# Strided attention rows loaded as 64 + 8 instead of 72, into a larger ring, with more batches held ahead

## The chip, the cores and the metric

The kernel runs on one core of one Trainium2 chip. Times are device microseconds (us) of that core. Most runs of a kernel agree within some tenths of a per cent; runs over 1.5% above the fastest of the same kernel are called slow and left out of comparisons. A ratio of two kernels is the mean time of one kernel's fast runs over that of the other's of the same rounds, so it is not quite the ratio of the medians that stand beside it. Its 95% interval is given.

Positions inside a run ("at 71.86 us") are counted from the start of the profiled span.

## The reference, cut to what matters

Eight heads of attention over 576 positions, eight batches: heads 0 to 3 attend to the last 32 positions ("local"), heads 4 to 7 to the positions with the same remainder by 32 ("strided"). The result goes through a spectral layer with 64 complex modes, each with a real and an imaginary weight matrix of 512 x 512 in f32, and a last matrix.

```python
mask_local = (rel >= 0) & (rel < stride)
mask_strided = (rel >= 0) & (pos[None, :] % stride == pos[:, None] % stride)
...
X = np.fft.rfft(x, axis=1)
Yr = einsum('bmd,mde->bme', Xr, w_r) - einsum('bmd,mde->bme', Xi, w_i)   # 64 modes
Yi = einsum('bmd,mde->bme', Xr, w_i) + einsum('bmd,mde->bme', Xi, w_r)
u = x + irfft(Y);  out = u + maximum(u @ w_ch, 0)
```

The weights are 134 MB of the 163 MB that the kernel reads. They are read once, in two halves (128 tiles, each for one mode and one half of the channels).

## The kernel before

GpSimd issues all large loads; they turn f32 into f16 on the way. In order of time: eight strided batches, eight local batches with the first 64 modes between their pieces, then the second 64 modes with the turns and premixes of the output, then the output.

```python
NWBUF = 12                                   # weight tiles
pin = tile_pool(name="pin", bufs=3)          # three batches of q, k, v

def load(i):                                 # i < 8: strided batch i; else local batch i - 8
    qn = pin.tile([128, 3, 2048], F16, tag="qn")
    for vi, src in ((2, v), (0, q), (1, k)):
        if i < B:      # 4 heads x 18 = 72 rows of 32 x 64 f32
            nc.gpsimd.dma_start(qn[0:72, vi, :],
                src[i, 4:8].rearrange("h (c r) d -> (h c) (r d)", r=32))
        else:          # 128 rows of 18 x 64
            nc.gpsimd.dma_start(qn[:, vi, 0:1152],
                src[i - B, 0:4].rearrange("h (cb i) d -> (h cb) (i d)", i=18))
...
load(0); load(1); load(2); w_fetch(2)
for b in range(B):                           # strided stage
    load(b + 3)
    w_fetch([3, 3, 2, 2, 2, 2, 1, 1][b])
    ...
for b in range(B):                           # local stage, with modes of the first half
    load(B + b + 3)
    ...
```

A mode multiplies with its tile and then fetches the tile that will take its place; modes 3 to 6 sit in guest tiles and fetch nothing. In the second half the turns and premixes ("work") lie between the modes, two a mode over the last `LATE` modes:

```python
LATE = 10
first = len(work) - 2 * LATE
for m in range(NM - 3):
    mode(1, m)                               # 16 matmuls with the weight tile, then w_fetch()
    if m < NM - 3 - LATE:
        upto = -(-first * (m + 1) // (NM - 3 - LATE))
    else:
        upto = first + 2 * (m - (NM - 4 - LATE))
    for w in work[n:upto]:
        w()
    ...
```

The softmax here doesn't subtract the row's maximum and nothing guards it: scores larger than these inputs give would overflow.

## Time and profile before

| | before |
|---|---|
| time, median of 4 runs | 443.22 us (442.81 to 445.03) |
| span of the profiled run | 440.9 us |
| last strided load landed | 74.96 us |
| last weights landed | 402.17 us |
| from there to the end | 38.75 us |

The landings are read from the trace: each load makes sixteen completions, read here as one for each of the sixteen DMA engines, and has landed with the last. The two landings divide the run. Up to 74.96 us the strided loads and the first weight tiles are moved, up to 402 the rest of the stream, and then only the output is left. The prediction below shows the slices, the windows and the chain of waits of this kernel.

### The profile page before, as it was taken

To read this page: it belongs to the slowest core of one execution; us is meant where nothing else is said; L and a number is where in the kernel's file an instruction comes from. 1 tells how busy PE (TensorE), PEld (TensorE's weight loads), DVE (VectorE), ACT (ScalarE), POOL (GpSimd) and SP (SyncE) were. 2 spreads that over 40 slices of the span, in tenths; PEclk is the share of its full clock that TensorE was granted. 3 is DMA by queue.
4 is the path that set the end of the run, shared out by engine and by line. 5 is a ranking of instruction groups with operands and counts; after the bars stand their busy time and mean duration, and the time that the engine had idled before them with its cause. 6 is when DMAs were issued, how large, how long until landed. Compare 5 with 4: busy or idle time off the path is not lost.

```text
span 440.9 us, 12290 instructions
## 1 busy us (share of the span) xinstructions
PE 335.6 (76%) x5284; PEld 240.4 (55%) x5284; DVE 215.9 (49%) x462; ACT 188.7 (43%) x353; POOL 181.1 (41%) x327
## 2 busy tenths in 40 slices
PE   2887778769899897875885567777685858987994
PEld 2766667648778765664663344444453535654441
DVE  3787868644435434150511034344334442763894
ACT  1685767554545553342441302123313402443882
POOL 5333333432544343533443443433434444420883
PEclk9998989697958995585865559596869778999999
DMA  8999999999999999999999999999999999992687
GB/s 186 183 201 201 200 196 204 211 211 208 198 211 212 211 212 212 212 211 212 213 210 211 212 211 213 213 211 212 211 198 207 213 211 212 212 212 44 263 329 268
DMA packets 30902, 92.35 MB, mean 209 GB/s; under 512 B 5952, under 2 KB 6848, under 8 KB 30848
## 3 DMA queue, kind: packets, MB, share of 16 engines
q0 software_dynamic: 26608, 81.28, 94.3%
q1 hardware_dynamic: 3440, 9.50, 5.7%
q8 instruction: 42, 0.69, 0.6%
q10 hardware_dynamic: 800, 0.77, 0.6%
q14 instruction: 12, 0.10, 0.1%
HBM read 163.37 MB, written 9.44 MB: 392 GB/s over the span
## 4 chain that ended last, share of the span: by engine, by line
DMA 58%; PE 28%; DVE 6%; issue 4%; ACT 3%; DVEq 0%; POOL 0%; POOLq 0%; ACTq 0%
DMA wt<-in_moe_w_i_dram 38%; DMA wt<-in_moe_w_r_dram 9%; DMA qn<-in_v_dram 5%; PE y L515 4%; DMA qn<-in_q_dram 4%; PE tp L363 3%; PE sc L613 2%; DMA qn<-in_k_dram 2%; PE v L860 2%; PE u L663 2%; PE v L648 2%; PE sc L409 1%; PE sc L482 1%; DVE xb L218 1%; PE sc L425 1%
## 5 line engine op out<-in xcount | busy, mean ns | idle before, releaser
L515 PE MATMUL y<-X,wt 128*128 128x16 f16 (+1 forms) x2048 | 82.8, 192 | 63.2 <-DMA wt<-in_moe_w_i_dram 60.1
L180 POOL DMA_DIRECT2D wt<-in_moe_w_r_dram x128 | 66.4, 519 | 131.0 <-DMA wt<-in_moe_w_r_dram 29.6
L515 PEld LDWEIGHTS <-wt 128*128 128x128 f16 (+1 forms) x2048 | 72.1, 103 | 76.7 <-issue 56.1
L180 POOL DMA_DIRECT2D wt<-in_moe_w_i_dram x126 | 65.3, 518 | 61.8 <-DMA wt<-in_moe_w_i_dram 38.8
L622 ACT ACTIVATE v<-sc 128x512 f16<-128x512 f32 x32 | 19.0, 597 | 88.8 <-PE sc L613 88.8
L613 PE MATMUL sc<-w_cp,xT 128*128 128x512 f16 (+1 forms) x160 | 49.8, 439 | 0.5 <-DVE xT L585 0.4
L439 ACT ACTIVATE PL<-sc 128x480 f16<-128x480 f32 (+1 forms) x48 | 27.6, 579 | 38.4 <-PE sc L425 38.0
L623 DVE COPY xo<-tp 128x512 f16<-128x512 f16 x32 | 22.1, 692 | 39.4 <-PE tp L621 39.4
L218 DVE TENSOR_TENSOR xb<-av,rec 90x256 f16<-90x256 f32 (+2 forms) x80 | 36.0, 450 | 2.8
L217 DVE RECIPROCAL rec<-av 90x4 f32<-90x4 f32 (+2 forms) x80 | 14.7, 184 | 43.0 <-PE av L454 30.1
L370 DVE COPY qT<-tp 128x576 f16<-128x576 f16 x16 | 12.1, 759 | 45.1 <-PE tp L363 45.1
L228 ACT ACTIVATE v<-tp 128x640 f16<-128x640 f16 (+1 forms) x24 | 19.4, 808 | 26.1 <-PE tp L397 22.8
L363 PE MATMUL tp<-cI_s,qn 64*64 64x64 f16 x864 | 27.5, 216 | 3.6 <-DMA qn<-in_q_dram 2.2
L328 ACT ACTIVATE PS<-sc 90x360 f16<-90x360 f32 (+1 forms) x48 | 22.7, 489 | 9.6 <-PE sc L321 9.2
L363 PEld LDWEIGHTS <-qn 64*64 64x64 f16 x864 | 21.8, 128 | 8.8 <-issue 3.5
L873 POOL TENSOR_TENSOR rl<-rl,xo 128x512 f32<-128x512 f32 x16 | 18.3, 1158 | 18.2 <-ACT rl L871 17.8
L890 DVE TENSOR_TENSOR osb<-u,rl 128x512 f32<-128x512 f32 x36 | 23.9, 689 | 2.5 <-PE u L663 0.7
L409 PE MATMUL sc<-cMl_s,cI_s 128*128 128x480 f16 (+1 forms) x48 | 22.6, 471 | 1.6 <-ACT X L228 1.6
L253 PE MATMUL tp<-cI_s,qn 72*128 72x72 f16 x256 | 14.8, 207 | 11.8 <-DMA qn<-in_v_dram 9.1
L482 PEld LDWEIGHTS <-xb 108*128 108x128 f16 (+2 forms) x176 | 17.3, 115 | 11.8 <-DVE xb L218 6.1
L425 PE MATMUL sc<-qT,kz 128*128 128x160 f16 (+1 forms) x160 | 22.7, 269 | 0.0
L565 DVE COPY xT<-tp 128x512 f16<-128x512 f16 x16 | 11.0, 689 | 23.4 <-DMA wt<-in_moe_w_i_dram 14.2
(94 smaller groups left out, 639.4 us busy)
## 6 DMA issues: line engine op xcount, KB each, us to landing
wt<-in_moe_w_r_dram POOLq DMA_DIRECT2D x128, 256.0 KB, 9.4
wt<-in_moe_w_i_dram POOLq DMA_DIRECT2D x126, 256.0 KB, 9.7
out_dram<-osb SPq DMA_DIRECT2D x14, 512.0 KB, 2.7
qn<-in_v_dram POOLq DMA_DIRECT2D x16, 288.0 KB, 10.7
qn<-in_q_dram POOLq DMA_DIRECT2D x16, 288.0 KB, 10.7
qn<-in_k_dram POOLq DMA_DIRECT2D x16, 288.0 KB, 11.0
out_dram<-osb SPq DMA_DIRECT2D x7, 128.0 KB, 2.5
out_dram<-osb SPq DMA_DIRECT2D x3, 256.0 KB, 3.2
```

The lines of the kernel that those rows point to most:

```text
L180: nc.gpsimd.dma_start(wt[ds(64 * ri, 64)], src[m, ds(256 * half, 256), :].rearrange("(p c) e -> p c e", c=4),)
L218: nc.vector.tensor_tensor(out=dst, in0=val.rearrange("p h (q c) -> p h c q", c=4), in1=rec[0:n, 0:pieces] .to_broadcast((n, pieces, 64)) . ...
L328: nc.scalar.activation(out=PS[0:n, ds(POFF[t], 4 * n)], in_=scp[0:n, 0 : 4 * n], func=ACTF.Exp, scale=SCALE,)
L363: nc.tensor.transpose(tp[ds(64 * hp, 64), ds(64 * i, 64)], qn[ds(64 * hp, 64), vi, ds(64 * (9 * g + i), 64)], idn[ds(64 * hp, 64), ds(64 * ...
L409: nc.tensor.matmul(scp[:, 0 : n * times].rearrange("p (h x) -> p h x", h=times), idn, mask_rows("cMl", n, times), start=True, stop=False,)
L425: nc.tensor.matmul(scp[:, ds(col, n)], kzs[par][:, hp, ds(s0, 128)], qTs[par][:, ds(s0, n)], start=False, stop=(i == len(todo) - 1),)
L439: nc.scalar.activation(out=dst, in_=src, func=ACTF.Exp, scale=SCALE)
L482: nc.tensor.matmul(xp[:, ds(192 * cp, 192)], xb[b][0:n, base + t, ds(128 * cp, 128)], F[0:n, t, :], start=(i == 0), stop=(i == len(tiles) ...
L515: nc.tensor.matmul(yv[:, mi, e, :], wt[pr, XC[c], ds(128 * e, 128)], Xh[half][pr, c, :, :, m], start=(c == 0), stop=(c == 3),)
L613: nc.tensor.matmul(vp[pr, :], xT[:, ch, cols], w_chs["cp"][:, ch, :], start=(ch == 0), stop=(ch == 3),)
L623: nc.vector.tensor_copy(out=xo[pr].rearrange("p (h q c) -> p h q c", h=2, c=4), in_=tp[pr, 0:512].rearrange("p (h c q) -> p h q c", h=2, c=4),
L890: nc.vector.tensor_tensor(out=osb[:, t % 2, :], in0=up, in1=rls[b, t][:, t % 2, :], op=AluOp.add)
```

## The change

Its intent: to give each DMA engine the same share of a strided load, and to keep more loads in hand. A strided tensor comes as 64 rows of its batch; its last 8 rows come with those of the next batch in one load of 8 partitions x 2 rows (here called the tail), every second batch. All of it lies in one ring of 12 tensors (four batches); local batches use two ring places each, six of them ahead. For the room, a weight tile is given up and the strided probabilities (PS) lie inside the local ones (PL), which costs one more fill with zeros.

```diff
-NWBUF = 12
+NWBUF = 11
...
-    PS = pat.tile([128, 2342], F16, name="PS")
+    PS = PL[:, ds(PS0, 2342)]
+    ring = pat.tile([128, 12, 2048], F16, name="ring")
...
+    def load_str(b):
+        for vi in (2, 0, 1):
+            nc.gpsimd.dma_start(
+                str_in(b, vi)[0:64],
+                SRC[vi][b, 4:8].rearrange("h (c r) d -> (h c) (r d)", r=32)[0:64],
+            )
+            if b % 2 == 0:
+                n = 3 * (b % 4) + SLOT[vi]
                 nc.gpsimd.dma_start(
-                    qn[0:72, vi, :],
-                    src[i, 4:8].rearrange("h (c r) d -> (h c) (r d)", r=32),
+                    ring[64:72, n : n + 4 : 3, :],
+                    SRC[vi][b : b + 2, 4:8].rearrange(
+                        "b h (c r) d -> (h c) b (r d)", r=32
+                    )[64:72],
                 )
...
-        load(b + 3)
-        w_fetch([3, 3, 2, 2, 2, 2, 1, 1][b])
+        if b < 5:
+            load_str(b + 3)
+        load_loc(*[(), (), (), (), (0,), (1, 2), (3,), (4, 5)][b])
+        w_fetch([3, 3, 2, 2, 2, 1, 1, 1][b])
...
-        load(B + b + 3)
+        load_loc(b + 6)
```

More of the change, by code (lines that the diff above doesn't have):

```diff
@@ L146 @@
     actx = ctx.enter_context(ExitStack())
-    pin = actx.enter_context(tc.tile_pool(name="pin", bufs=3))
+    pin = actx.enter_context(tc.tile_pool(name="pin", bufs=1))
     pat = actx.enter_context(tc.tile_pool(name="pat", bufs=1))
+    ring = pat.tile([128, 12, 2048], F16, name="ring")
     qTs = [pat.tile([128, 1152], F16, name=f"qT{i}") for i in range(2)]
@@ L152 @@
     vT = pat.tile([128, 1216], F16, name="vT")
-    PS = pat.tile([128, 2342], F16, name="PS")
     PL = pat.tile([128, 4160], F16, name="PL")
+    PS0 = 4160 - 2342
+    PS = PL[:, ds(PS0, 2342)]
     v16 = [pat.tile([128, 12, 132], F16, name=f"v16_{i}") for i in range(2)]
     GUEST = {3: ("Y0", 0), 4: ("Y0", 1), 5: ("X0", 0), 6: ("X0", 1)}
-    GUEST |= {16: ("YT", 0), 17: ("YT", 1)}
+    GUEST |= {15: ("YT", 0), 16: ("YT", 1)}
     guests = {}
@@ L189, in w_ch_fetch, with str_in, loc_in, load_loc @@
         w_chs["n"] = w_ch
-    qns = {}
-    def load(i):
-        if i >= 2 * B:
-            return
-        qn = pin.tile([128, 3, 2048], F16, tag="qn", name="qn")
-        for vi, src in ((2, v), (0, q), (1, k)):
-            if i < B:
+    SRC = {2: v, 0: q, 1: k}
+    SLOT = {2: 0, 0: 1, 1: 2}
+    def str_in(b, vi):
+        return ring[0:72, 3 * (b % 4) + SLOT[vi], :]
+    def loc_in(b, vi):
+        t = ring[:, ds(2 * (b % 6), 2), :].rearrange("p n x -> p (n x)")
+        return t[:, ds(1152 * vi, 1152)]
+    def load_str(b):
[6 more added lines that the diff above has]
+                n = 3 * (b % 4) + SLOT[vi]
                 nc.gpsimd.dma_start(
-                    qn[0:72, vi, :],
-                    src[i, 4:8].rearrange("h (c r) d -> (h c) (r d)", r=32),
-                )
-            else:
+                    ring[64:72, n : n + 4 : 3, :],
+                    SRC[vi][b : b + 2, 4:8].rearrange(
+                        "b h (c r) d -> (h c) b (r d)", r=32
+                    )[64:72],
+                )
+    def load_loc(*bs):
+        for b in bs:
+            if b >= B:
+                return
+            for vi in (2, 0, 1):
                 nc.gpsimd.dma_start(
-                    qn[:, vi, 0:1152],
-                    src[i - B, 0:4].rearrange("h (cb i) d -> (h cb) (i d)", i=18),
+                    loc_in(b, vi),
+                    SRC[vi][b, 0:4].rearrange("h (cb i) d -> (h cb) (i d)", i=18),
                 )
-        qns[i] = qn
     def v_cols(i):
@@ L233, in str_q @@
     def str_q(b, g):
-        qn, qT = qns[b], qTs[b % 2]
+        qn, qT = str_in(b, 0), qTs[b % 2]
         tp = psum("tp", half=True)
@@ L238, in str_q @@
                 tp[:, ds(72 * i, 72)],
-                qn[0:72, 0, ds(128 * (8 * g + i), 128)],
+                qn[:, ds(128 * (8 * g + i), 128)],
                 idn[0:72, 0:72],
@@ L247, in str_turn @@
     def str_turn(b, vi, j):
-        qn = qns[b]
+        qn = str_in(b, vi)
         a, z = JG[j]
@@ L254, in str_turn @@
                 tp[:, ds(72 * i, 72)],
-                qn[0:72, vi, ds(128 * (a + i), 128)],
+                qn[:, ds(128 * (a + i), 128)],
                 idn[0:72, 0:72],
@@ L358, in loc_turn @@
     def loc_turn(b, vi, g):
-        qn, par = qns[B + b], b % 2
+        qn, par = loc_in(b, vi), b % 2
         tp = psum("tp", half=True)
@@ L364, in loc_turn @@
                     tp[ds(64 * hp, 64), ds(64 * i, 64)],
-                    qn[ds(64 * hp, 64), vi, ds(64 * (9 * g + i), 64)],
+                    qn[ds(64 * hp, 64), ds(64 * (9 * g + i), 64)],
                     idn[ds(64 * hp, 64), ds(64 * hp, 64)],
@@ L676 @@
     psum_pools(tp=3, sc=3, av=2)
-    load(0)
+    load_str(0)
     const_load(nc.scalar, "cI", "cM6", "cM5", "cFs")
-    load(1)
+    load_str(1)
     const_load(nc.sync, "cMl", "cFl", "cA")
-    load(2)
+    load_str(2)
     w_fetch(2)
@@ L733 @@
         if b == 1:
-            nc.vector.memset(PL, 0.0)
+            nc.vector.memset(PL[:, 0:PS0], 0.0)
     str_values(B - 1, 4)
     str_values(B - 1, 5)
+    nc.vector.memset(PS, 0.0)
     dft(B - 1, 1)
```

## The prediction

> **What bounds the kernel now.** I read the page first (slices, chain), then the chain in order of time, then the busy time in windows, and last the completions of single loads in the trace.
>
> ```profile
> DMA  8999999999999999999999999999999999992687
> GB/s 186 183 201 201 200 196 204 211 211 208 198 211 212 211 212 212 212 211 212 213 210 211 212 211 213 213 211 212 211 198 207 213 211 212 212 212 44 263 329 268
> ...
> DMA 58%; PE 28%; DVE 6%; issue 4%; ACT 3%; DVEq 0%; POOL 0%; POOLq 0%; ACTq 0%
> ```
>
> Each slice is 11.0 us. The DMA is at 9 tenths in all slices from the second to the 36th, and the chain of waits is 58% DMA. The rate is 210 to 213 GB/s (bytes written to SBUF, half of what is read, since the loads turn f32 into f16) on most of the way, but 183 to 204 in the first seven slices, which are the strided attention. The windows show it finer (last columns: granted clock, DMA share, GB/s):
>
> ```profile
> 40.00:50.00 10.00, 8.56 (x159) 7.15 (x157) 8.27 (x25) 8.06 (x17) 3.79 (x8) 1.00 1.03 198
> 50.00:60.00 10.00, 7.78 (x142) 6.50 (x143) 8.29 (x23) 7.95 (x19) 3.66 (x7) 1.00 1.03 200
> 60.00:70.00 10.00, 7.51 (x111) 6.57 (x111) 6.33 (x18) 5.72 (x13) 3.71 (x8) 0.83 1.03 197
> ...
> 80.00:90.00 10.00, 7.35 (x147) 6.37 (x147) 6.90 (x17) 4.87 (x10) 3.79 (x8) 0.66 1.08 210
> ...
> 110.00:120.00 10.00, 9.06 (x210) 7.36 (x210) 5.00 (x10) 5.48 (x11) 5.77 (x11) 1.00 1.03 196
> 120.00:130.00 10.00, 9.03 (x182) 7.70 (x183) 3.48 (x8) 4.52 (x7) 4.15 (x8) 0.60 1.09 212
> ```
>
> DMA share 1.03 against 1.07 to 1.09 means that some of the 16 DMA engines stand idle in the strided stage, although loads are always queued. The chain in time says what the end hangs on:
>
> ```profile
> 71.86 10.22 DMA qn<-in_q_dram
> 82.12 1.17 PE tp L363 x36
> ...
> 147.62 9.85 DMA wt<-in_moe_w_r_dram
> ...
> 361.70 9.63 DMA wt<-in_moe_w_i_dram
> 371.46 0.65 PE y L515 x16
> 372.11 0.86 PE sc L613 x4
> ```
>
> Up to 82 us it is mostly loads, from 82 to 147 PE (local attention with the first modes), from 147 to 371 weight loads alone, then compute with the last modes. Setting each mode's first matmul beside the landing of its weights: mode 0 starts 75 us after its weights landed, mode 33 1.7 us, and from mode 34 (158.7 us) to the end of the stream most start within 0.05 to 0.7 us of the landing. So the PE-bound stretch is absorbed by the weights held ahead, and what sets the end is **when the load stream has moved all its bytes**. The last weights land at 402.2 us, and 38.7 us of modes, spectra and output follow.
>
> **How a strided load runs.** Completions of each load, read one by one from the trace: a load counts 16 completions. Of the eight strided loads issued first, the eighth gets its first completion at 7.3 us, its second at 11.1, and the other fourteen between 18.8 and 19.7. One engine gets none of the 72 rows, one gets two, fourteen get five each: 14 x 5 + 2 = 72. A weight load (64 rows of 4 KB) completes every 1.237 us, four rows an engine, so 0.309 us a row. An even strided load would take 72 / 16 x 0.309 = 1.39 us; five rows are 1.55. From 59.65 to 69.42 us three strided and four weight loads end: (9.77 - 4 x 1.24) / 3 = 1.60 us each. The uneven shares thus cost about 1.60 - 1.39 = 0.21 us x 24 loads = **5.1 us**. The light engines can't use the time: GpSimd's loads signal eight semaphores in turn, and each waits for the load eight before it, so no more than eight are outstanding.
>
> **What the Trainium skill says.** "DMA: Bandwidth & Descriptors", section "Why a DMA increments its semaphore by 16 and not by 1": as a rule the engine count k is the largest number up to 16 that divides the slowest dimension, the k engines being taken from a round-robin cursor; but GpSimd gives some copies k = 16 with partitions/16 rounded up per engine. The trace agrees with the exception: 72 rows go as 14 x 5 + 2 (the rule would give 12 x 6). For the new tail load, whose slowest dimension is 8, the rule gives eight engines in rotation, the exception one partition each on the same eight; no load of the kernel before has that shape. "SBUF — State Buffer", section "Door 1: The DMA port swizzle": partitions 64 to 67 share one of 16 write ports, 68 to 71 another, about 27 GB/s each. Nothing in this trace isolates that: the 64-row weight loads, which that page confines to eight ports (about 218 GB/s), reach 212 but alternate between halves.
>
> **The change, part by part.**
> - *64 rows.* Each of 24 main loads has four rows an engine, like a weight load: 24 x 1.24 = 29.8 us of stream.
> - *Tails.* 12 loads of 8 partitions x 2 rows of 4 KB. Spread or rotated they cost 16 rows / 16 x 0.309 = 0.31 us on average, 3.7 in all; with main loads 33.5, against 24 x 1.60 = 38.4 now: **-4.9 us**. Always on the same eight engines they cost 2 rows, 0.62 us, 7.4 in all: 37.2, only **-1.2 us**, since those eight would carry 4 + 4 + 2 = 10 rows per pair and tensor, as fourteen carry now.
> - *GpSimd issue.* 12 more at 0.53 us, 6.4 us; GpSimd is 41% busy and waits for the semaphores anyway: nothing.
> - *Ring of four batches instead of three.* A strided load no longer waits for the batch just transposed. Those waits did not empty the queue (eight outstanding), so nothing on its own.
> - *Six local batches ahead, one weight tile less.* Before the first refill there are now 17 tiles and 6 batches instead of 18 and 4: two batches (3 loads x 1.40 us each) more, one tile (2.47 us) less, 5.9 us more work in hand. Now there is a pause of issues, 104.7 to 110.0 us (modes 3 to 6 free no tile), and completions slip there: 196 instead of 212 GB/s for 10 us, **0.75 us**. With more queued it should go. The weights of modes 30 to 50 come later relative to the locals, but the sum at mode 63 is the same. Total bytes do not change. Eleven tiles are still far more than the four that eight outstanding loads fill.
> - *PS inside PL.* One fill of 2342 columns at the stage's end; 4160 columns take 1.79 us now, so about 1.0 us on DVE (38% to 69% busy from 80 to 100 us), in the stretch that the held weights absorb: nothing.
>
> Sum: 4.9 + 0.75 = 5.65 us if the tails rotate, 1.95 us if they do not. At the end everything hangs on the stream: mode 115 starts 0.14 us after its landing, and from there the compute chain has its fixed length, so a gain of the stream is passed on whole.
>
> **Rivals.**
> 1. *Tails always on the same eight engines*: 443.3 - 2 = 441.4. For it: the 72-row loads follow the rounding exception. Against: the tail has another form (two counts, 8 and 2).
> 2. *The two ports of partitions 64 to 71 hold up the tails.* By that page's rate, 64 KB over 2 x 27.2 GB/s is 1.2 us a tail instead of 0.31, if all engines write it at once: up to 12 x 0.9 = 10.7 us lost, so 443.3 - 5.65 + 10.7 = 448. Against: engines are spread by 2 to 8 us between first and last completion of a load, and an average over a pair of batches is far under the ports' rate. I take part of it, perhaps 1 to 2 us.
> 3. *Compute takes over.* In the strided stage DVE and ACT are at about 80%; if the stage can't run faster, the loads still run ahead into ring and weight tiles, so it becomes the end only if PE stays behind past mode 34. Then the time is 443. Against: PE is only 71% busy from 200 to 250 us.
> 4. *The loads in a wrong order or a hidden wait between them*: neighbouring loads into one tensor with a stride of three slots might be ordered behind each other's landing (about 10 us each, six or eight times, with an emptied queue): 460 or more. Nothing in the profile speaks for it.
>
> **Range and chances.** Rotation (-5.65) and fixed engines (-2) about evenly, a little less for ports: -4.3, so 439.0. The best case with the other start-up slack gone (the first 20 us at 184 GB/s also carry the constants) is about -8, 435.3; a full port loss partly paid back, or compute taking over, gives 443.5. A gain over 2% would need -8.9 us, more than the losses that I find in the stage: 6%. Slower by 2% needs the fourth rival or the full second one: 2%.
>
> **What would show it.** Right: the first seven slices near 208 to 212 GB/s, DMA share 1.07 in windows of the strided stage; main loads completing every 1.24 to 1.3 us; no dip at 110 us; the last weights landing at about 398 us with the same 38 to 39 us after it; weights as the main part of the chain from about 150 us. Tails on eight fixed engines would show as the share staying near 1.04 and eight early completions per load. Ports would show as tails whose packets take well over the 0.32 us of a 4 KB row now. The prediction is wrong if GpSimd waits for landings of tails, if the stage after 98 us leaves the DMA idle, or if the stretch after the last landing grows.

## The result, and the profile after

The changed kernel takes 438.94 us (median of 4 runs, 438.3 to 439.67) against 443.22; the ratio is 0.9896 (0.9865 to 0.9928). Two later comparisons gave 0.9888 and 0.9916. The forecast was 439.0.

The slices and the chain of the changed kernel's page:

```profile
DMA  8999999999999999999999999999999999990687
GB/s 186 211 211 212 211 213 209 211 210 211 213 211 212 213 208 211 213 212 211 211 212 211 213 212 210 213 213 210 201 211 212 211 212 213 211 192 15 264 324 277
...
DMA 74%; PE 15%; DVE 4%; issue 4%; POOL 1%; ACT 0%; DVEq 0%; POOLq 0%
```

The stage that ran at 183 to 204 GB/s runs at 209 to 213 from the second slice on, and the dip near 110 us (198) is gone. The thirty-sixth slice has begun to empty (192) and the thirty-seventh stands at 15, where it was 212 and 44: the stream ends earlier. The windows that answer to those in the prediction:

```profile
40.00:50.00 10.00, 7.83 (x146) 6.58 (x144) 8.35 (x23) 7.46 (x18) 4.68 (x10) 1.00 1.07 213
50.00:60.00 10.00, 7.98 (x147) 6.59 (x143) 8.30 (x24) 8.00 (x18) 4.88 (x10) 1.00 1.06 211
60.00:70.00 10.00, 8.08 (x148) 6.72 (x145) 8.27 (x24) 7.92 (x18) 4.59 (x9) 1.00 1.07 210
...
110.00:120.00 10.00, 8.67 (x249) 7.39 (x241) 5.84 (x10) 5.74 (x11) 3.98 (x8) 1.00 1.07 213
```

The DMA share (next to last column) is 1.06 to 1.07 where it was 1.03. Over the whole run PE, DVE and ACT are busy for 338.0, 215.6 and 188.6 us, where it was 335.6, 215.9 and 188.7: the same compute, better fed.

Below are the landings of both kernels, in us.

| | before | after | gain |
|---|---|---|---|
| last strided load landed | 74.96 | 70.14 | 4.8 |
| weights of mode 115 landed | 371.33 | 366.52 | 4.8 |
| last weights (mode 127) landed | 402.17 | 396.36 | 5.8 |
| first matmul of mode 127 | 402.41 | 399.05 | 3.4 |
| span | 440.9 | 437.8 | 3.1 |

So the stream gained 4.8 us in the strided stage, still 4.8 at mode 115 and 5.8 at its end (the prediction's favourable case was 5.65), and the kernel did not get all of it. Before, the last mode started 0.24 us after its weights. Now it starts 2.7 us after them: PE and DVE are behind. (The profiled run of the changed kernel, 439.67 us, was the slowest of its four; that of the kernel before took 442.69. So the spans are 3.1 us apart and the medians 4.3.) The chain of the changed kernel in time, cut to where this happens:

```profile
366.65 0.65 PE y L536 x16
...
387.27 1.22 PE sc L634 x3
388.49 0.43 PE tp L642 x4
388.91 0.47 PE y L536 x16
389.39 1.71 PE sc L634 x4
391.10 0.22 PE tp L642 x4
391.32 0.86 PE sc L634 x4
```

From 366.65 us (mode 115) on, no load is in the chain: it is the modes (L536), the premixes (L634, L642) and DVE's copies. The chain was as long as that before, too (30.95 us from mode 115 to mode 127, now 32.40). The difference is the clock: the premix matmuls at 387 and 389 us take 1.22 and 1.71 us, those at 391 us 0.86. The two stretches as windows, first the kernel before and then the changed one:

```profile
371.40:402.40 31.00, 27.02 (x354) 17.69 (x355) 18.97 (x39) 11.85 (x20) 8.78 (x17) 1.00 0.95 189
```

```profile
366.60:399.10 32.50, 28.57 (x356) 18.31 (x357) 18.91 (x38) 11.84 (x20) 8.76 (x17) 0.95 0.88 176
```

PE is busy for 27.02 us at a granted clock of 1.00 in the one and for 28.57 us at 0.95 in the other. A repeat of the changed kernel drew 0.95 again (32.4 us), another 1.00 (31.0 us):

```profile
367.60:398.60 31.00, 27.12 (x354) 17.76 (x355) 19.29 (x39) 11.92 (x21) 8.76 (x17) 1.00 0.92 184
```

Ten fast profiles have this stretch with the same work in it. In five the clock is 1.00 and it takes 30.9 to 31.0 us, in the other five the clock is 0.95 and it takes 32.4 to 32.6, whether the stream ends at 396 or at 402 us. So which clock it gets is chance, as far as these runs show.

Even at full clock the chain of 31 us is longer than the 29.7 us in which twelve tiles come (two loads of 1.237 us each). Before, that did not show at the last mode: the stream stumbled twice in its last 16 us (two loads landed 2.10 and 2.69 us after their predecessors instead of 1.24) and ended no earlier than the compute. Its chain has no load after mode 115 either. So of the 5.8 us, 1.0 is only that these late loads are missing now, in a stretch where compute sets the end. The 4.8 us that the stream had gained by mode 115 are passed on, less 1.45 us for the clock: 3.4. Why the two loads came late is not known; the other two profiles with whole 72-row loads need 30.7 and 30.9 us for the twelve tiles too, the other fast ones 29.7 to 29.9.

### The profile page after: what moved, and what is told of

It is laid out like the page before. It is cut to its first block, busy times and chain, and to the rows that moved or that the text cites. A ratio compares the mean times of both kernels' runs of the same rounds, so it can differ in the third digit from the quotient of the medians.

```text
span 437.8 us, 12314 instructions
## 1 busy us (share of the span) xinstructions
PE 338.0 (77%) x5284; PEld 240.9 (55%) x5284; DVE 215.6 (49%) x463; ACT 188.6 (43%) x353; POOL 186.8 (43%) x339
## 4 chain that ended last, share of the span: by engine, by line
DMA 74%; PE 15%; DVE 4%; issue 4%; POOL 1%; ACT 0%; DVEq 0%; POOLq 0%
DMA wt<-in_moe_w_i_dram 54%; DMA wt<-in_moe_w_r_dram 12%; DMA ring<-in_v_dram 4%; DMA ring<-in_q_dram 4%; PE sc L634 3%; PE v L884 2%; PE v L669 2%; PE u L684 2%; PE y L536 1%; DVE yy L663 1%; PE u L903 1%; PE tp L313 1%; POOL wt L183 1%; PE tp L642 1%; DVE xT L586 1%
## 5 line engine op out<-in xcount | busy, mean ns | idle before, releaser
L536 PE MATMUL y<-X,wt 128*128 128x16 f16 (+1 forms) x2048 | 82.2, 192 | 59.0 <-DMA wt<-in_moe_w_i_dram 57.1
L536 PEld LDWEIGHTS <-wt 128*128 128x128 f16 (+1 forms) x2048 | 72.0, 103 | 72.7 <-issue 51.7
L634 PE MATMUL sc<-w_cp,xT 128*128 128x512 f16 (+1 forms) x160 | 52.5, 459 | 0.5 <-DVE xT L606 0.4
L349 ACT ACTIVATE PL<-sc 90x360 f16<-90x360 f32 (+1 forms) x48 | 22.8, 490 | 9.8 <-PE sc L342 9.1
L384 PE MATMUL tp<-cI_s,ring 64*64 64x64 f16 x864 | 26.1, 211 | 1.0 <-DVE qT L391 0.6
L384 PEld LDWEIGHTS <-ring 64*64 64x64 f16 x864 | 20.7, 123 | 6.2 <-issue 3.4
L634 PEld LDWEIGHTS <-xT 128*128 128x128 f16 (+1 forms) x160 | 14.8, 110 | 14.9 <-issue 7.2
L446 PEld LDWEIGHTS <-kz 128*128 128x128 f16 x160 | 16.7, 118 | 11.3 <-issue 8.8
L274 PE MATMUL tp<-cI_s,ring 72*128 72x72 f16 x256 | 15.1, 207 | 10.1 <-DMA ring<-in_v_dram 7.7
## 6 DMA issues: line engine op xcount, KB each, us to landing
ring<-in_q_dram POOLq DMA_DIRECT2D x8, 288.0 KB, 10.7
```

The lines of the kernel that those rows point to most:

```text
L349: nc.scalar.activation(out=PS[0:n, ds(POFF[t], 4 * n)], in_=scp[0:n, 0 : 4 * n], func=ACTF.Exp, scale=SCALE,)
L384: nc.tensor.transpose(tp[ds(64 * hp, 64), ds(64 * i, 64)], qn[ds(64 * hp, 64), ds(64 * (9 * g + i), 64)], idn[ds(64 * hp, 64), ds(64 * hp, ...
L446: nc.tensor.matmul(scp[:, ds(col, n)], kzs[par][:, hp, ds(s0, 128)], qTs[par][:, ds(s0, n)], start=False, stop=(i == len(todo) - 1),)
L536: nc.tensor.matmul(yv[:, mi, e, :], wt[pr, XC[c], ds(128 * e, 128)], Xh[half][pr, c, :, :, m], start=(c == 0), stop=(c == 3),)
L634: nc.tensor.matmul(vp[pr, :], xT[:, ch, cols], w_chs["cp"][:, ch, :], start=(ch == 0), stop=(ch == 3),)
```

## The experiments

Twelve runs were made, on several chips; each is compared with the kernel before on its own chip (median 443.7 to 444.2 us). All results were correct. The table has what the profiled run of each shows, with the row packet's mean over 20 to 75 us (a row of 2048 f16 is one packet of 4096 bytes; in the two kernels with two pieces these are the rows of weights alone, as a strided row makes two packets there).

| run | median us | ratio (95%) | last strided landing | mean packet, ns | last weights landed | last mode behind them |
|---|---|---|---|---|---|---|
| before (first profile) | 443.22 | 1 | 74.96 | 335.8 | 402.17 | 0.24 |
| changed, again | 439.23 | 0.9888 (0.9862 to 0.9914) | 69.89 | 324.2 | 396.18 | 2.80 |
| changed, third | 439.39 | 0.9916 (0.9888 to 0.9944) | 70.19 | 324.1 | 397.15 | 1.47 |
| 72 rows in the ring | 443.49 | 0.9988 (0.9964 to 1.0013) | 75.10 | 332.1 | 401.86 | 1.96 |
| split only | 442.17 | 0.9959 (0.9936 to 0.9982) | 72.72 | 332.1 | 399.40 | 1.37 |
| one-row tails | 441.68 | 0.9946 (0.9924 to 0.9969) | 72.70 | 333.8 | 399.33 | 1.35 |
| dummies between tails | 444.41 | 1.0001 (0.9968 to 1.0033) | 77.41 (slow run) | 339.3 (slow run) | 403.93 (slow run) | 3.60 (slow run) |
| changed, even spread | 437.49 | 0.9853 (0.9828 to 0.9878) | 69.55 | 324.3 | 395.95 | 0.13 |
| before, even spread | 443.47 | 0.9985 (0.996 to 1.0011) | 74.34 | 332.5 | 402.03 | 0.14 |
| two pieces | 443.76 | 1.0007 (0.9987 to 1.0027) | 75.20 | 346.1 | 401.74 | 2.94 |
| two pieces, even spread | 442.73 | 0.9989 (0.9973 to 1.0006) | 76.68 | 346.5 | 403.21 | 0.13 |
| locals as before | 441.18 | 0.9961 (0.9921 to 1.0) | 70.07 | 324.2 | 398.44 | 1.36 |
| 80 rows | 442.01 | 0.9938 (0.9892 to 0.9984) | 72.35 | 324.2 | 399.22 | 2.80 |

### The changed kernel again

> The changed kernel itself, once more, beside the others on one chip. Measured before: 438.94 us against 443.22, and in its profile the last weights land at 396.36 us against 402.17 (5.8 us earlier), but the last mode starts 2.7 us after its weights landed instead of 0.24. Theory A (the stream's gain is steady, the loss after it is how fast PE runs in the last 30 us): again 438 to 440 us, last landing 396 to 397, last mode 2 to 4 us behind it. Rival (the profiled run was unlucky): last mode less than 1 us behind, and the time nearer to 437.

> The changed kernel, to be compared on one chip with the three kernels beside it: 438 to 440 us, last landing about 396 us, last mode 2 to 4 us behind it.

The stream ends at 396.18 and 397.15 us and the last mode is 2.80 and 1.47 us behind. The two runs differ in the granted clock of the last stretch (0.95 and 1.00), as told above. The loss at the end is steady, its size is not; the rival (under 1 us behind) is out.

### The split undone

```diff
             nc.gpsimd.dma_start(
-                str_in(b, vi)[0:64],
-                SRC[vi][b, 4:8].rearrange("h (c r) d -> (h c) (r d)", r=32)[0:64],
+                str_in(b, vi),
+                SRC[vi][b, 4:8].rearrange("h (c r) d -> (h c) (r d)", r=32),
             )
-            if b % 2 == 0:  ... (the tail)
```

> The changed kernel with the 64 + 8 split undone: each strided tensor comes as one load of 72 rows again, everything else (ring of four batches, six local batches ahead, 11 weight tiles, fill of PS at the end of the stage) is kept. Theory A (the even shares carry the gain): strided loads complete every 1.6 us again, 40 to 80 us is back at about 200 GB/s, the last weights land at 401 to 402 us, time 441.5 to 443.5; the pause near 110 us stays away, worth 0.75 us. Rival B (the gain is the ring and the work in hand): last landing stays near 397 and the time at 439.

443.49 us, a ratio of 0.9988: no different from the kernel before. The stage from 20 to 70 us, first the changed kernel and then this one:

```profile
20.00:70.00 50.00, 39.96 (x697) 33.58 (x695) 40.74 (x112) 38.19 (x83) 23.31 (x45) 0.97 1.06 211
```

```profile
20.00:70.00 50.00, 40.46 (x681) 33.38 (x679) 39.14 (x108) 37.11 (x80) 19.15 (x37) 0.93 1.03 201
```

211 GB/s falls back to 201, and the last landings of both kinds are those of the kernel before within 0.3 us. So ring, six batches and eleven tiles bring nothing by themselves; the split carries the gain. Rival B is out.

### The split alone, with tails of one row

```diff
-                nc.gpsimd.dma_start(
-                    qn[0:72, vi, :],
-                    src[i, 4:8].rearrange("h (c r) d -> (h c) (r d)", r=32),
-                )
+                rows = src[i, 4:8].rearrange("h (c r) d -> (h c) (r d)", r=32)
+                nc.gpsimd.dma_start(qn[0:64, vi, :], rows[0:64])
+                nc.gpsimd.dma_start(qn[64:72, vi, :], rows[64:72])
```

> The kernel before with only the loads split: 64 rows, then 8 rows of the same batch, into its own three tiles, 12 weight tiles, locals as before. Theory A: the strided stage runs at 208 to 212 GB/s, last landing 4 to 5 us earlier than before (397 to 398 us), the pause of issues near 105 to 110 us is still there (it may cost more, as less or no more work is in hand), time 439 to 440.5. Rival B (ring and work in hand): no earlier than 401 us, time 442 to 443.5.

The gain is about half of what I expected: 442.17 us, last landing 399.40. The old kernel can't hold the tails of two batches at once, so each tail has eight rows of one batch here. The next run shows that it is this form, and not the missing ring, that halves the gain.

### One-row tails in the changed kernel

```diff
-            if b % 2 == 0:
-                n = 3 * (b % 4) + SLOT[vi]
-                nc.gpsimd.dma_start(ring[64:72, n : n + 4 : 3, :], ... )
+            nc.gpsimd.dma_start(
+                str_in(b, vi)[64:72],
+                SRC[vi][b, 4:8].rearrange("h (c r) d -> (h c) (r d)", r=32)[64:72],
+            )
```

> The changed kernel with 24 tails of 8 rows of one batch instead of 12 of 8 x 2 rows. If eight engines are taken in turn, two tails of one row do what one of two rows does: last landing within 0.5 us of the changed kernel, time within 0.7 us (438.3 to 439.7), with 12 more issues that cost nothing. Rival (a tail costs a fixed time per load, or always lies on the same engines): 12 more tails at 0.3 us each, last landing 3 us later or more, time about 441.

441.68 us and a last landing at 399.33, 3.15 us later than in the changed kernel on the same chip: the first theory falls and the rival's number stands. The completions of a 64-row load tell which of the rival's two reasons is right. They are listed from the trace; the last of the four lines is the first load of a later experiment.

```
kernel, load issued at            its sixteen completions (us)
before, 5.04                      7.32, 11.07, then fourteen from 18.81 to 19.67
changed, 12.25 (64 rows)          sixteen from 17.82 to 19.48, no gap over 0.37
one-row tails, 13.45 (64 rows)    eight from 17.67 to 17.79, eight from 18.86 to 19.38
two pieces, 1.35 (72 rows)        four from 4.89 to 5.14, twelve from 6.52 to 7.49
```

With one-row tails the engines fall into two groups of eight, one group ahead of the other, and the distance from first to last completion grows to 4.0 us by the 18th tensor. The distance falls to 2.3 to 3.1 us for the last six tensors. A cost per load would hit all engines alike. So tails of one row fall on the same eight engines each time, which then have 4 + 1 = 5 rows for every tensor, as fourteen engines had before. The tails of 8 x 2 rows do not: with 12 of them the spread stays between 1.5 and 2.9 us through the stage, and the stage ends 2.8 us earlier. Always on the same eight, 12 tails of two rows would cost those eight just what 24 of one row do.

That is the prediction's favourable case by its effect, but a tail spread over all sixteen engines, a row each, would have the same effect. The trace does not name the engine of a packet; still, the completions tell the two apart. With one-row tails the first completion of a tail comes 0.15 to 0.19 us after the first of its main load, in 23 of 24 tails: the engine that is ahead never gets a row of the tail. With two-row tails it comes, from the third to the twelfth, 0.17, 0.50, 0.17, 0.50, 0.18, 0.62, 0.18, 0.59, 0.21 and 0.57 us after it: the engine that is ahead gets no row and two rows in turn. The four other profiles with the changed kernel's strided loads alternate as well. So the engines change from tail to tail.

### Dummies between the tails

```diff
+    scr = pat.tile([128, 12, 16], F16, name="scr")
...
+                nc.gpsimd.dma_start(
+                    scr[0:8, 3 * (b // 2) + SLOT[vi], :], v[0, 0, 0:8, 0:16]
+                )
```

> The changed kernel with a dummy load of 8 rows of 64 bytes after each tail, into a scratch tensor that nothing reads. If the eight engines of a load are taken from a cursor that moves on by eight, the dummies take one half of the engines each time and all real tails fall on the other half: those carry 4 + 4 + 2 = 10 rows per pair of batches and tensor, 2 rows more than if alternated over two tails as 1 on average, 12 x 0.31 = 3.7 us of stream. Expected then: completions of one load spread over 4 us and more by the end of the strided stage (2.2 us in the changed kernel), rate near 203 to 206 GB/s, last landing at about 400 us, time 441.5 to 443. Rival (the tail's 16 rows lie on all 16 engines, or always on the same eight whatever comes between): landing within 0.7 us of the changed kernel's 396.4, time within 1 us of it.

This run does not answer its question. It is as slow as the kernel before (ratio 1.0001), but probably not by the reason that it was to test: the dummies have the one-row form, which by the run above does not move on, and they fill the queue. GpSimd waits for the load eight before, and with a tail and a dummy after each main load only two or three of those outstanding from 17 to 20 us are main loads. The engines then seem to run dry: the load issued at 19.56 us lands on all sixteen engines within 0.81 us, as after a pause. Its profile: slow (448.7 us), so its landings are not compared, and that the full queue costs the time is not shown. It does show that small loads take places in the queue of eight.

### 72 rows in two pieces

```diff
-    ring = pat.tile([128, 12, 2048], F16, name="ring")
+    ring = pat.tile([128, 12, 2080], F16, name="ring")
...
+                ring[0:72, 3 * (b % 4) + SLOT[vi], :].rearrange(
+                    "p (k x) -> p k x", k=2)[:, :, 0:1024],
+                SRC[vi][b, 4:8].rearrange("h (c k r) d -> (h c) k (r d)", k=2, r=16),
...  (no tails; the transposes skip the gap of 16)
```

> The changed kernel without tails: each strided tensor is again one load of 72 rows, but each row lies in two pieces of 1024 in SBUF with a gap of 16 between them, so that the load has two counts (72 and 2) like the tail of the changed kernel, and not one. Theory D (a load with two counts goes to the largest number of engines up to 16 that divides 72, that is 12 with 6 rows each, and the 12 move on from load to load; a load with one count is cut into 5 rows for each of fourteen engines): on average 4.5 rows an engine, strided stage at 207 to 212 GB/s, last landing 396 to 398 us, time 438.3 to 440. If the 12 did not move on, twelve engines would carry 6 rows every time and the stage would be at 175 GB/s, last landing 407 us, 448 us. Rival E (two counts change nothing, 5 rows on fourteen engines): as with whole rows, last landing 401 to 402, time 443 to 444.

Half of theory D holds. The first load shows four early completions and twelve later ones (list above): twelve engines, not fourteen and two. And the spread stays between 1.0 and 4.7 us through the stage, so the twelve move on; had they not, the last landing would have come at 407 us by the estimate above. But the time is that of the kernel before (443.76 us, last landing 401.74), because the packets take longer: half a row takes 173 ns in the median, so a row 346 instead of 324, and 605 of 3,400 half-row packets between 5 and 75 us take over 25 ns more than that. Even shares on average were not enough.

The same with the even spread of the work:

> The same with turns and premixes spread evenly over the modes of the second half. If theory D holds and the even spread is worth what it was in the changed kernel (0.9853 of before against 0.9888), this is 1 to 2.5 us faster than the two pieces alone: 436.5 to 438, last mode under 1 us after its weights. If the even spread only seemed faster by chance between two chips, no difference to it.

442.73 us, 0.8 us under the two pieces by the ratios (0.9989 against 1.0007, intervals overlapping); the last mode is 0.13 us behind its weights. That is the expected direction, but less than the 1 to 2.5 us expected and not clear of noise; 436.5 to 438 us was out of reach, as the stream had not become faster.

### Local batches as before

```diff
-        load_loc(*[(), (), (), (), (0,), (1, 2), (3,), (4, 5)][b])
+        load_loc(*[(), (), (), (), (), (0,), (1,), (2,)][b])
...
-        load_loc(b + 6)
+        load_loc(b + 3)
```

> The changed kernel with the local batches loaded where the kernel before loads them (three ahead instead of six), split and ring and 11 weight tiles kept. If the work in hand is worth what I predicted (0.75 us for the pause of issues near 105 to 110 us, perhaps 1 to 2 us now that the stage ends its loads 5 us earlier and has one weight tile less): the pause is back, slower by 0.5 to 2 us than the changed kernel, last landing 396.8 to 398.5. If the six batches ahead are worth nothing: the same within 0.4 us.

The pause is back. GpSimd issues nothing from 98.60 to 105.00 us. The windows of this kernel around it (the changed kernel has 211 and 213 GB/s there):

```profile
100.00:110.00 10.00, 9.89 (x247) 8.29 (x244) 3.90 (x9) 6.67 (x13) 3.96 (x8) 0.93 0.99 182
110.00:120.00 10.00, 8.23 (x192) 6.85 (x189) 4.69 (x9) 4.57 (x8) 3.88 (x9) 0.75 1.04 200
```

The last weights land at 398.44 us against 397.15 on the same chip, 1.3 us later, and the median is 1.8 us higher, with overlapping intervals. So the batches ahead are worth more with the split than without (0.3 us of landing in the run with 72 rows): the stream that has become faster runs out of free buffers sooner.

### 80 rows

This kernel has the 72-row loads and the ring, and eight rows more per load, so that all sixteen engines have five.

```diff
-                str_in(b, vi),
-                SRC[vi][b, 4:8].rearrange("h (c r) d -> (h c) (r d)", r=32),
+                ring[0:n, 3 * (b % 4) + SLOT[vi], :],        # n = 80, for the last batch 72
+                rows[ds((b * 8 + 4) * NCB, n)],
```

> The kernel with whole 72-row loads and the ring (as in the earlier run that undid the split), but each strided load of batches 0 to 6 takes eight rows more (from the next heads, into partitions that nothing reads), so 80 rows: 16 engines with 5 rows each, 0.69 MB more in all. It separates the two things that differ between 72 and 64 rows. In the strided stage of the kernels with 72-row loads a row packet takes 332 to 338 ns on average, against 324 with 64 rows. Theory F (blocks of five partitions make packets slow, whatever the balance): mean 332 ns or more again, last strided landing at 75 us or later, no light engines (completions of one load within 3 us). Theory G (the engines that run ahead disturb the others): with all engines even the mean falls to 324 to 327 ns and the last strided landing comes at 73.5 to 74.5 us, at 1.55 us a load. In both cases 16 engines have five rows where fourteen had them, so the time stays within 1.5 us of the kernel before (443.86), although more bytes are moved.

Theory G, and more of it than I expected. With 0.69 MB **more** to move, the last strided load lands at 72.35 us instead of 75.10 and the last weights at 399.22 instead of 401.86. The row packet takes 324.2 ns in the mean instead of 332.1, without a change in the size of a block. The windows from 20 to 70 us of this kernel, to be held against 201 GB/s and a share of 1.03 with 72 rows:

```profile
20.00:70.00 50.00, 40.26 (x683) 33.35 (x680) 40.49 (x112) 37.41 (x82) 19.31 (x37) 0.93 1.06 212
```

The rate by itself shows little: twelve loads with eight extra rows of 4 KB in these 50 us are 8 of the 11 GB/s between the two kernels. The landings count: 2.75 us at the last strided load, 1.8 us at the weights of mode 115 (369.34 against 371.13 us). These are one profile each, on two chips, where three of the changed kernel differ by 1.0 us at mode 115, and the intervals of the two times overlap. So 1.8 to 2.75 us of the loss were not the longer share of five rows, which is still there, but came with having two light engines, far ahead of the others. The rest, 2.2 us from 72.35 to 70.14 us or 2.8 us at mode 115, goes with five rows against four and a half. How engines out of step slow the packets is not shown by these runs. Nor is packet time alone the loss: one-row tails have slow packets (333.8 ns) and a landing like that of 80 rows.

### The work of the second half spread evenly

```diff
-    LATE = 10
+    LATE = 0
```

> The changed kernel, with the turns and premixes spread evenly over all modes of the second half (1.2 a mode) instead of two a mode over the last ten. In the changed kernel the modes 117 to 126 fall behind their weights by 0.3 to 5.8 us, since a mode with two items takes PE about 2.9 us and weights come every 2.47. Theory A (the stream's gain is lost to this stretch of compute): the last mode starts under 1 us after its weights, time 2 to 3 us less than the changed kernel's (436 to 437). Rival C (PE's granted clock sets it: more work earlier lowers the clock later, or the output stage starts at a lower clock): no gain or a loss, 438.5 to 440.5.

> The kernel before with the same even spread. There the last mode starts 0.24 us after its weights, so the stretch of compute hides behind the stream: theory A expects no gain here, 442.5 to 444 us, last landing 402. Rival C (the even spread is better or worse by itself through the clock): it moves by as much as in the changed kernel, the same sign.

In the changed kernel the last mode now starts 0.13 us after its weights, and the chain of waits has no compute left before the end of the stream. These are its pieces in time (the changed kernel's chain had no load after 366.65 us):

```profile
376.41 9.63 DMA wt<-in_moe_w_i_dram
386.04 0.28 issue
386.32 9.62 DMA wt<-in_moe_w_i_dram
395.95 0.14 issue
396.08 0.65 PE y L536 x16
396.74 0.02 issue
```

The time is 437.49 us, a ratio of 0.9853, against 0.9888, 0.9896 and 0.9916 of the changed kernel: by the ratios 1.6 to 2.8 us less, about what was expected. It stood on another chip than those three, and its interval overlaps two of theirs at the edges; in the profile the step is plain, in the time it is likely. In the kernel before the same edit moves nothing that is clear of noise (0.9985, 443.47 us). In its profile the last twelve tiles took 30.85 us, as long as the compute at full clock, so there was little to gain. That fits theory A; rival C, by which the spread would help both alike, is not supported, though the interval leaves room for 1.8 us. It is not the faster stream that makes the compute late: with 72 rows in the ring, where the stream ends as late as before, the last mode is 1.96 us behind (clock 0.95). The changed kernel with the even spread is the fastest of all that were run.

## Why the prediction was right or wrong

The time was right to 0.1 us, and that is luck. The forecast weighed a favourable and an unfavourable case of the stream and passed the gain on whole; in fact the favourable case came true in the strided stage, and a part was lost at the end. Nor does its sum hold: -5.65 and -2 about evenly are -3.8, and "a little less for ports" makes the gain smaller, not the -4.3 that was written.

- **"What sets the end is when the load stream has moved all its bytes"**: right for the strided stage and up to mode 115. Undoing the split gives back all the time. From mode 115 on compute sets the end, in the kernel before too.
- **"Up to 82 us it is mostly loads"**: misread. Loads are about 48% of that part of the chain, 17% in its first 41 us and 80% from there to 82. That the stage hangs on the loads is shown by the 72-row run and not by the chain.
- **"The uneven shares thus cost about 0.21 us x 24 loads = 5.1 us"**: right in size (4.8 us by the last strided landing; 5.2 against the 72-row load in the same ring), but it is two things. The 80-row run shows 1.8 to 2.75 us of it without any engine having fewer than five rows. I put the difference between 1.60 us measured and 1.55 calculated down to the shares as well, and by the calculation shares would be 0.155 x 24 = 3.7 us; they were 2.2 to 2.8.
- **"Rotation (-5.65) and fixed engines (-2) about evenly"**: rotation. One-row tails, which stay on eight engines, end the stream 3.15 us later than two-row tails, and the 4.8 us of the strided stage match the -4.9 calculated for rotation. That the last weights landed 5.8 us earlier, near the favourable sum of 5.65, is chance: 1.0 us of it are the two late loads of the kernel before.
- **"With more queued it should go"** (the pause, 0.75 us): it went, but between the two kernels its gain does not show (4.8 us at the last strided load and 4.8 at mode 115). Its size was too small beside the split: 1.3 us by the landing when three batches are held ahead instead of six.
- **"So a gain of the stream is passed on whole"**: this step failed in part. What the stream gains up to mode 115 is passed on, but the length of the chain from there is not fixed: about 31 us at a granted clock of 1.00 and 32.5 at 0.95, which cost 1.45 us in the profile. And I counted the gain at the last landing, where it no longer matters: twelve tiles take 29.7 us, less than the chain, and stream and chain ended together before only because two loads came late. Now the chain ends 1.5 to 2.8 us after the stream, more when the clock is 0.95, and the stretch after the last landing grew from 38.75 to 41.43 us, which the forecast itself had named as a sign that it is wrong. The even spread takes that away.
- **Rivals.** The two ports of the tails, estimated at up to 10.7 us: between 20 and 75 us, 15 of 2,593 row packets take over 350 ns (242 of 2,645 before), so nothing holds them up (with only twelve tails, this says nothing against the rates of the ports). Compute that takes over: not in the strided stage or in the middle, where from mode 24 on most modes start within 1 us of the landing of their weights, but at the end, where the forecast named it only past mode 34 in general. A hidden wait between tails: no wait of GpSimd in the first 100 us was longer than 2.1 us, where the landing of a load takes about 8. The single fill of PS took 1.03 us and showed nowhere.

## What to carry to other kernels

Where loads bound a kernel, look at the sixteen completions of single loads: engines that finish far ahead of the others mean uneven shares, and they can cost time beside the longest share itself (with eight useless rows a load the last strided load landed 2.75 us earlier). When a stream gets faster, check where it stops setting the end: here 31 us of compute against 30 us of loads ended both kernels, so that only what the stream had gained before that stretch counted, and moving that work earlier took the delay out of the profile. Count loads and not bytes where the number outstanding is limited.

## What the Trainium skill lacked or had wrong

- "DMA: Bandwidth & Descriptors", section "Why a DMA increments its semaphore by 16 and not by 1": it says that GpSimd gives "some direct copies" k = 16 with the partitions rounded up per engine, but not which. Here loads with one count (72 or 8 rows) behave that way (completions at 7.32, 11.07 and fourteen from 18.81 us for 72 rows; 8 rows on the same eight engines), and loads with two counts follow the rule with engines in rotation (72 x 2: twelve engines, four early completions at 4.89 to 5.14 us; 8 x 2: the first completion comes 0.17 to 0.21 and 0.50 to 0.62 us after that of the main load in turn).
- The same page has nothing on engines out of step. With 80 rows on sixteen engines the last strided load landed at 72.35 us and a row packet took 324.2 ns in the mean, with 72 rows on fifteen at 75.10 us and 332.1 ns, with the same five rows on the busiest engine.
- No page has a measured time for a load split into half rows. Here a packet of 2048 bytes written took 173 ns in the median, one of 4096 bytes 324, so 7% more per byte.
